# A spectral-filter and token-mixing kernel on Trainium2: a leaner first stage, and six filter scans moved into the filter stage

## The chip, the cores and the metric

The kernel runs on one core of one Trainium2 chip. The core has five engines that run their own instruction streams side by side: TensorE (PE, matrix products into PSUM, with its weight loads as PEld), VectorE (DVE), ScalarE (ACT), GpSimd (POOL) and SyncE (SP, which here only issues transfers). They wait for one another through semaphores, and each takes its instructions strictly in its own order: an instruction that waits holds back all that stands behind it on that engine. The metric is the device time of one execution in microseconds (us). Three runs of the kernel before gave a median of 1017.25 us (1016.85 to 1018.95).

## The reference

The input x has S = 2048 tokens by D = 640 channels. Two kinds of layer alternate, each twice, and each adds its result to x:

```python
def _A_ref(x, w_r, w_i):
    X = rfft2(x);  X = X * (w_r + 1j * w_i)          # filter: 2048 x 321 complex numbers
    return irfft2(X, s=(S, D))

def _B_ref(x, w1, b1, w2, b2):                        # MLP over the token axis, F = 1728
    u = gelu(einsum("bsd,sf->bdf", layernorm(x), w1) + b1)
    return transpose(einsum("bdf,fs->bds", u, w2) + b2)

x = x + _A_ref(_layernorm(x), w_r, w_i)
x = x + _B_ref(_layernorm(x), w1, b1, w2, b2)
x = x + _A_ref(_layernorm(x), w_r, w_i)
x = x + _B_ref(_layernorm(x), w1, b1, w2, b2)
```

## The kernel before, in words

The two-dimensional transform is done as matrix products with tables of cosines and sines, in pairs of float16 parts (a high part and a low part, which carries what the high one lost by rounding). The program is written in stages: the first stage (in `run`), and then twice: the filter stage `a1`, the inverse transform `a2`, and the MLP (`b1st`, `b2nd`).

**The first stage** works on 16 rows of tiles (128 tokens by 640 channels). It is pipelined by hand: step i of the loop `for i in range(NJ + 6)` loads x of row i+3, computes the mean and variance `mv` of row i on DVE, v (variance plus epsilon, ACT), r (its inverse root, POOL), nm (the negative mean, ACT) and nb (nm times r, POOL) of row i-1, the normalised z of row i-2 (ACT), the first fold of row i-3 (`a0_fold1`: `eo`, sums and differences of the two halves of z, POOL), the second fold of row i-4 (`a0_fold2`: `f`, DVE), the float32 products with the table tM of row i-5 (PE), and the split of the result into the float16 parts s1h (ACT) and s1l (DVE) of row i-6. Both folds end with a small copy of two columns that have no partner. `eo` and `f` have two buffers each. Every z is a fresh tile, whose two pad columns POOL clears.

Between those, the first stage reads the filter: for each of its 16 groups a **scan** loads the group's filter (`w`, 321 KB, on SP's queue) and lets ACT sum its squares into one column of `xq` (the tile `jw` takes the squares, which nobody reads). From all of `xq`, `scale_x` in group 0 of the filter stage makes the scales `sx` and a correction `cxe`: a product of `xq` with the identity `eye` on PE turns the columns into rows, DVE takes the maxima (`xm`), spreads them (`xb`), a second product with `eye` turns them back, and a chain of small DVE steps (`xqq`, `qi`, `sx`, `xof`, `cxe`) makes powers of two of them.

**The filter stage** works in groups g = 0 to 15. In group g stand, in this order: the products d of group g+1 (PE), the inverse products i of g-3, the products s of g (PE, from ph and pl), then xh, xl of g-2, the filter products ta and tb of g-1 (DVE, which read s's result in PSUM, the scale sx and the filter w), their sums sa, sb (POOL), the split ph (ACT) and pl (DVE) of the d result of g+1, and Yh (ACT), Yl (DVE) of the i result of g-3. In groups 4 to 7 small steps for the scale of the MLP's bias (`scale_b`) are put between; one of them is a product of `sqb` with a column of ones on PE, which goes to a spare column of the newest s result's PSUM tile.

**What sets the order.** Around the change nothing is reordered: the work is pinned in the order in which the program issues it, each engine's part of it in that order. All transfers named here go through SP's one queue. All instructions of the engines record the same line (L59, in the kernel after it L60), that of a helper, so that one goes by tiles.

Of the kernel before, what the change touches and what calls it, by code (L numbers as in the profile page):

```python
# [22 lines left out]
NX = 5  # L23
LAST = '''
# [42 lines left out]
class Layers:  # L67
# [156 lines left out]
    def scan_x(self, pool, g):  # L224

        w = self.t(pool, [128, 2, NL], F32, "w", 3)
        self.nc.sync.dma_start(w, self.A["w"][g])
        junk = self.t(pool, [128, 2, NL], BF16, "jw", 1)
        return lambda: self.T.activation(junk, w, AF.Square, accum_out=self.xq[:, g:g + 1])

    def scale_x(self, pool):

        V, mm = self.V, self.PE.matmul
        ps = self.big()
        mm(ps[:NG, 0, :128], self.xq, self.eye, start=True, stop=True)
        m = pool.tile([NG, 1], F32, name="xm")
        V.tensor_reduce(m, ps[:NG, 0, :128], op=ALU.max, axis=mybir.AxisListType.X)
        yield
        b = pool.tile([NG, 128], F32, name="xb")
        V.tensor_copy(b, m.to_broadcast([NG, 128]))  # L240
        mm(ps[:, 1, :NG], b, self.eye[:NG, :NG], start=True, stop=True)
        yield
        q = pool.tile([128, NG], F32, name="xqq")
        V.tensor_scalar(q, ps[:, 1, :NG], SMALL, XS ** -2, op0=ALU.max, op1=ALU.mult)
        i = self.pow2(q, self.sx)
        V.tensor_scalar(q, i, EC * 0.5 / TS, None, op0=ALU.mult)
        yield
        of = pool.tile([128, NG], F32, name="xof")
        V.tensor_reduce(of, self.eye.rearrange("p (g a) -> p g a", g=NG), op=ALU.add, axis=mybir.AxisListType.X)
        V.tensor_tensor(of, of, q, op=ALU.mult)  # L250
        V.tensor_reduce(self.cxe, of, op=ALU.add, axis=mybir.AxisListType.X)
# [64 lines left out]

    def a0_fold1(self, z, sv=False):
# [10 lines left out]
    def a0_fold2(self, eo, between=lambda: None, gp=False):  # L328

        V, W = self.V, self.G if gp else self.V  # L330
# [10 lines left out]
        W.tensor_copy(f[:, 607:640:32], eo[:, 160:482:321])  # L341
# [92 lines left out]
    def a1(self, first):  # L434
# [232 lines left out]
        spare = lambda c: lambda: ps2[max(ps2)][:, 1, c:c + 1]  # L667
        for g in range(NG - 3):
            for op in group(g):
                do(op)  # L670
                if op == "pl%d" % (g + 1) and 9 <= g < 13:
                    self.wsplit(0, quarter(g - 9)[0], hi=False, part=quarter(g - 9)[1])
                if op == "d1" and first:
                    sx = self.scale_x(p)
# [9 lines left out]
            if g > 0 and g + 2 < NG:  # L684
                w[g + 2] = wload(g + 2)
            if g == 3:
# [984 lines left out]
    def run(self):  # L1671
# [9 lines left out]
        scans = []  # L1681
        x, st, z, eo, f, pv, vs, nms = ({} for _ in range(8))

        def load(i):
            if i < NJ:
                x[i] = self.t(self.pT, [128, D], F32, "xt", 6)
                self.lastld = nc.sync.dma_start(x[i], self.xs[0][i])
                if i % 4 == 0:
# [273 lines left out]
```

## Time and profile before

| | |
|---|---|
| median of 3 runs | 1017.25 us (1016.85 to 1018.95) |
| the profiled execution | 1017.07 us, of which the span of the profile is 1015.3 us |
| PE busy | 969.4 us (95% of the span), 8235 products |
| DVE, ACT, POOL busy | 781.8 us (77%), 576.5 us (57%), 300.0 us (30%) |
| chain that ended last | PE 36%, DVE 13%, ACT 6%, POOL 3%, DMA 2% of the span |
| mean granted clock of PE | 0.979 |
| transfers | 176.45 MB, mean 174 GB/s |

How to read what follows: a row of a timeline has the start (us from the span's start), the duration, the engine, the line, the operation, its output and input tiles with their sizes, how many instructions the row joins, and in brackets how long the engine had been idle before it and what ended that. A row of a table of windows has each engine's busy time in that stretch, the number of its instructions in brackets, then the clock that PE was granted (1.00 is full speed), the share of the DMA engines' time and what they moved.

### The profile page before, as it was taken

The numbers are of one execution on the slowest core, as the hardware profiler recorded it, in microseconds if no ns is written. First come the engines' busy times: TensorE is split into PE (matmuls) and PEld (weight loads), VectorE is DVE, ScalarE is ACT, GpSimd is POOL, SyncE is SP. The second block draws the span as 40 slices with busy tenths as digits, with TensorE's granted clock in tenths as the row PEclk, the third lists the DMA queues.
The fourth block names the chain that finished last, engine by engine and source line by source line (L and its number), as shares of the span: only waits on it lengthen the run. The fifth ranks groups of instructions, "written<-read, shape, count | busy, mean of one in ns | idle before, by whom it ended". The sixth has DMA issues, their size and how long they took to land.

```text
span 1015.3 us, 20992 instructions
## 1 busy us (share of the span) xinstructions
PE 969.4 (95%) x8235; PEld 721.2 (71%) x8235; DVE 781.8 (77%) x1493; ACT 576.5 (57%) x890; POOL 300.0 (30%) x502
## 2 busy tenths in 40 slices
PE   4889999999999999999999799999999999999998
PEld 3778777677777667777777688776777777677776
DVE  7978978988777784666666689789965557998885
ACT  5857668687666455555553377685643454544531
POOL 6937857412212201222222277574000000000000
PEclk9599999999999999999999999999999999999999
DMA  7865356557657546464423455365444446755411
GB/s 232 279 185 164 115 178 219 206 187 255 236 195 250 186 124 246 139 193 146 126 89 117 126 181 181 105 229 204 159 156 164 145 142 228 245 177 190 153 45 53
DMA packets 67259, 176.45 MB, mean 174 GB/s; under 512 B 7996, under 2 KB 15320, under 8 KB 67160
## 3 DMA queue, kind: packets, MB, share of 16 engines
q1 hardware_dynamic: 59384, 146.92, 45.1%
q0 software_dynamic: 7776, 28.20, 7.5%
q8 instruction: 64, 1.05, 0.4%
q14 instruction: 35, 0.29, 0.1%
HBM read 127.24 MB, written 47.84 MB: 172 GB/s over the span
## 4 chain that ended last, share of the span: by engine, by line
PE 36%; DVE 13%; ACT 6%; POOL 3%; issue 3%; DMA 2%; SPq 0%; ACTq 0%; DVEq 0%; POOLq 0%
PE ps L59 36%; DVE wl L59 3%; DMA xt<-x 2%; DVE st L59 2%; DVE xt L59 1%; POOL eo L59 1%; DVE f L59 1%; ACT wh L59 1%; ACT xt L59 1%; ACT z L59 1%; DVE s1l L59 1%; ACT junk L59 1%; POOL xt L59 1%; DVE Yl L59 1%; DVE S L59 1%
## 5 line engine op out<-in xcount | busy, mean ns | idle before, releaser
L59 PEld LDWEIGHTS <-wh 128*128 128x128 f16 x2602 | 251.9, 98 | 103.6 <-issue 5.0
L59 PEld LDWEIGHTS <-wl 128*128 128x128 f16 x1610 | 157.5, 98 | 66.0 <-DVE wl L59 2.8
L59 PE MATMUL ps<-ul,wh 128*128 128x320 f16 x448 | 133.9, 301 | 0.6 <-DVE ul L59 0.6
L59 PE MATMUL ps<-uh,wl 128*128 128x320 f16 x448 | 133.9, 301 | 0.1
L59 PE MATMUL ps<-uh,wh 128*128 128x320 f16 x416 | 124.8, 300 | 1.6 <-DVE s L59 1.6
L59 PE MATMUL ps<-hl,wh 128*128 128x320 f16 x496 | 102.2, 299 | 0.9 <-DVE hl L59 0.9
L59 PEld LDWEIGHTS <-wo 128*128 128x128 f16 x756 | 73.9, 98 | 29.4 <-DVE wo L59 0.8
L59 DVE SCALAR_TENSOR_TENSOR wl<-raw,s,wh 128x896 f16<-128x896 f32 (+2 forms) x64 | 75.0, 1176 | 12.9 <-ACT wh L59 12.7
L59 ACT ACTIVATE junk<-raw 128x896 bf16<-128x896 f32 (+1 forms) x60 | 59.5, 991 | 44.2 <-DMA raw<-w 44.0
L59 POOL TENSOR_TENSOR r<-v,mh 128x1 f32<-128x1 f32 x64 | 36.4, 569 | 158.4 <-DVE nm L59 149.0
L59 PE MATMUL ps<-tDi,Yh 128*128 128x322 f16 x320 | 71.3, 300 | 0.2
L59 DVE TENSOR_TENSOR f<-eo 128x256 f32<-128x256 f32 (+1 forms) x124 | 39.1, 368 | 40.7 <-POOL eo L59 40.1
L59 ACT ACTIVATE wh<-raw,s 128x896 f16<-128x896 f32 (+2 forms) x68 | 67.2, 1010 | 2.3 <-DVE s L59 1.6
L59 POOL TENSOR_TENSOR xt<-xt,ec 128x320 f32<-128x320 f32 x64 | 52.5, 842 | 34.2 <-DVE xt L59 34.0
L59 ACT ACTIVATE z<-xt,nb,r 128x640 f32<-128x640 f32 x31 | 28.5, 919 | 57.6 <-POOL z L59 45.3
L59 PE MATMUL ps<-ph,tS 128*128 128x321 f16 (+2 forms) x288 | 58.5, 286 | 1.3 <-DVE tb L59 1.3
L59 PE MATMUL ps<-u,wo 128*128 128x320 f16 x420 | 59.0, 299 | 0.5 <-DVE wo L59 0.5
L59 DVE BATCH_NORM_STATS2 st<-xt 128x6 f32<-128x320 f32 x126 | 55.3, 480 | 5.2 <-DMA xt<-x 4.5
L59 PE MATMUL ps<-hha,wh 128*128 128x320 f16 x288 | 58.1, 299 | 0.9 <-DVE wh L59 0.9
L59 POOL TENSOR_TENSOR eo<-z 128x320 f32<-128x320 f32 x62 | 53.3, 881 | 17.0 <-ACT z L59 15.1
L59 PE MATMUL ps<-tM,f 128*128 128x128 f32 x160 | 39.5, 426 | 19.6 <-DVE f L59 19.6
L59 PE MATMUL ps<-tDi,Yl 128*128 128x322 f16 x192 | 55.7, 299 | 1.7 <-DVE Yl L59 1.7
(251 smaller groups left out, 2376.6 us busy)
## 6 DMA issues: line engine op xcount, KB each, us to landing
xt<-x SPq DMA_DIRECT2D x79, 320.0 KB
raw<-w SPq DMA_DIRECT2D x32, 512.0 KB
w<-w SPq DMA_DIRECT2D x48, 321.0 KB
x<-xt SPq DMA_DIRECT2D x47, 320.0 KB
raw<-w SPq DMA_DIRECT2D x32, 448.0 KB
raw<-w2z SPq DMA_DIRECT2D x32, 448.0 KB
w1S<-sp POOLq DMA_DIRECT2D x20, 512.0 KB, 3.7
out<-xt SPq DMA_DIRECT2D x15, 320.0 KB
```

Source lines behind the costliest of these rows:

```text
L59: i = f(*a, **k)
```

## The change

1. In the first stage, the two small copies go to ACT: a new function `a0_eo` takes the place of `a0_fold1`, and `a0_fold2` is called with `act=True`. nm falls away; nb is made by one POOL step from the mean and r. The z tiles are two fixed ones, whose pads are cleared once.
2. The order on ACT within a step is now s1h, z, copy of eo, v, copy of f, scan; row 0 is folded, and its products are issued, one step sooner (`soon`); the first part of the table tM is loaded behind x of row 2 instead of row 0.
3. The first stage holds ten scans, one in every second step and two behind the loop. The other six are done in the groups 0 to 5 of the filter stage: their loads on SP behind the group's loads, their ACT work at the group's end.
4. `scale_x` is done in two parts: columns 0 to 9 in group 0, where all of it stood, and columns 10 to 15 in group 6. There the first product with `eye` and the maximum stand behind s6, the spread and the second product behind ta5, the powers behind Yl3, all in spare columns of s6's PSUM tile; `xof` and `cxe` end that group.

ACT in the first stage, one step of the loop before (s1h to the scan's `jw`):

```order
L59 ACTIVATE s1h_195<-ps_430 128x80x8
L59 ACTIVATE nm_474<-mv_449 128x1
L59 ACTIVATE v_473<-mv_449,eps 128x1
L59 ACTIVATE z_487<-xt_282,nb_457,r_455 128x640
L59 ACTIVATE jw_422,xq<-w_420 128x642
```

and two steps of it now, one without and one with a scan:

```order
L60 ACTIVATE s1h_195<-ps_406 128x80x8
L60 ACTIVATE z_220<-xt_282,nb_432,r_430 128x640
L60 ACTIVATE eo_452<-z_219 128x2
L60 ACTIVATE v_456<-mv_424,eps 128x1
L60 ACTIVATE f_461<-eo_412 128x2
L60 ACTIVATE s1h_195<-ps_446 128x80x8
L60 ACTIVATE z_219<-xt_306,nb_472,r_470 128x640
L60 ACTIVATE eo_487<-z_220 128x2
L60 ACTIVATE v_491<-mv_464,eps 128x1
L60 ACTIVATE f_496<-eo_452 128x2
L60 ACTIVATE jw_476,xq<-ws_474 128x642
```

nm is gone, v stands behind z, and the copies of eo and f are in ACT's row.

ACT at the beginning of the filter stage, before (the last scan of the first stage, ph of groups 0, 1 and 2, xh of group 0):

```order
L59 ACTIVATE jw_858,xq<-w_856 128x642
L59 ACTIVATE ph_929<-ps_904 128x321 x2
L59 ACTIVATE ph_964<-ps_935 128x2x321
L59 ACTIVATE ph_1032<-ps_1009 128x2x321
L59 ACTIVATE xh_219_878<-ta_1026 128x2x321
```

and now:

```order
L60 ACTIVATE jw_764,xq<-ws_762 128x642
L60 ACTIVATE ph_845<-ps_820 128x321 x2
L60 ACTIVATE ph_887<-ps_857 128x2x321
L60 ACTIVATE jw_853,xq<-ws_851 128x642
L60 ACTIVATE ph_954<-ps_931 128x2x321
L60 ACTIVATE jw_856,xq<-ws_854 128x642
L60 ACTIVATE xh_175_794<-ta_948 128x2x321
```

A scan stands ahead of ph of group 2, and another ahead of the first xh.

DVE in group 6, before (ta and tb of group 5, pl of group 7, Yl of group 3, ta of group 6):

```order
L59 SCALAR_TENSOR_TENSOR ta_1445<-ps_1333,sx,w_1180 128x642
L59 SCALAR_TENSOR_TENSOR tb_1447<-ps_1333,sx,w_1180 128x642
L59 SCALAR_TENSOR_TENSOR pl_1452<-ps_1375,ph_1451 128x2x321
L59 SCALAR_TENSOR_TENSOR Yl_872<-ps_1392,Yh_871 128x96x4 x2
L59 SCALAR_TENSOR_TENSOR ta_1533<-ps_1429,sx,w_1274 128x642
```

and now, up to the first of the small steps on xqq:

```order
L60 TENSOR_REDUCE xm_1379<-ps_1365 6x1
L60 SCALAR_TENSOR_TENSOR ta_1384<-ps_1268,sx,w_1110 128x642
L60 COPY xb_1386<-xm_1379 6x128
L60 SCALAR_TENSOR_TENSOR tb_1389<-ps_1268,sx,w_1110 128x642
L60 SCALAR_TENSOR_TENSOR pl_1394<-ps_1311,ph_1393 128x2x321
L60 SCALAR_TENSOR_TENSOR Yl_788<-ps_1328,Yh_787 128x96x4 x2
L60 TENSOR_SCALAR xqq<-ps_1365 128x6
```

The maximum xm stands ahead of ta of group 5, the copy between ta and tb, and xqq behind Yl.

PE in group 6, before (the last product of s6, the product with ones, the first product of d8):

```order
L59 MATMUL ps_1429<-ph_1355,tS_198 128x321
L59 LDWEIGHTS ones
L59 MATMUL ps_1429<-sqb_278_1371,ones 128x1
L59 LDWEIGHTS s1h_195
L59 MATMUL ps_1463<-tD_197,s1h_195 128x160
```

and now, behind the last product of s6, with the semaphore on which each waits:

```order
L60 MATMUL ps_1365<-eye,xq 6x128 [waits Activation_49]
L60 MATMUL ps_1365<-eye,xb_1386 128x6 [waits DVE_49]
L60 LDWEIGHTS ones
L60 MATMUL ps_1365<-sqb_246_1307,ones 128x1 [waits DVE_49]
L60 LDWEIGHTS s1h_195
L60 MATMUL ps_1416<-tD_197,s1h_195 128x160 [waits PE_49]
```

Two products that depend on ACT and DVE stand between s6 and the product with ones, all three in s6's PSUM tile.

The diff, cut to its core:

```diff
-        w = self.t(pool, [128, 2, NL], F32, "w", 3)
+        w = self.t(pool, [128, 2, NL], F32, "ws", 2)
...
-    def scale_x(self, pool):
...
+    def scale_x(self, pool, cs, at=None):
+
+        V, mm, n = self.V, self.PE.matmul, cs.stop - cs.start
+        if not cs.start:
+            self.xqq = pool.tile([128, NG], F32, name="xqq")
+            ps = self.big()
+            at = (lambda: ps[:, 0, :128]), (lambda: ps[:, 1, :n])
+        a = at[0]()[:n]
+        mm(a, self.xq[:, cs], self.eye, start=True, stop=True)
+        m = pool.tile([n, 1], F32, name=f"xm{n}")
+        V.tensor_reduce(m, a, op=ALU.max, axis=mybir.AxisListType.X)
         yield
+        b = pool.tile([n, 128], F32, name=f"xb{n}")
+        V.tensor_copy(b, m.to_broadcast([n, 128]))
+        a = at[1]()[:, :n]
+        mm(a, b, self.eye[:n, :n], start=True, stop=True)
         yield
+        q = self.xqq[:, cs]
+        V.tensor_scalar(q, a, SMALL, XS ** -2, op0=ALU.max, op1=ALU.mult)
+        i = self.pow2(q, self.sx[:, cs])
         V.tensor_scalar(q, i, EC * 0.5 / TS, None, op0=ALU.mult)
         yield
+        if cs.stop == NG:
...
+    def a0_eo(self, z):
+
+        G = self.G
+        eo = self.t(self.pT, [128, 646], F32, "eo", 2)
+        v2 = lambda a, o, w: a[:, o:o + 2 * w].rearrange("p (a b) -> p a b", a=2)[:, :, 0:160]
+        za, zb = v2(z, 1, 161), v2(z, 321, 160)
+        G.tensor_tensor(v2(eo, 1, 161), za, zb, op=ALU.add)
+        self.lastpool = G.tensor_tensor(v2(eo, 322, 161), za, zb, op=ALU.subtract)
+        self.T.activation(eo[:, 0:162:161], z[:, 0:162:161], AF.Copy)
+        return eo
...
-        W.tensor_copy(f[:, 607:640:32], eo[:, 160:482:321])
+        if act:
+            self.T.activation(f[:, 607:640:32], eo[:, 160:482:321], AF.Copy)
+        else:
+            V.tensor_copy(f[:, 607:640:32], eo[:, 160:482:321])
...
-        spare = lambda c: lambda: ps2[max(ps2)][:, 1, c:c + 1]
+        spare2 = lambda c, e: lambda: ps2[max(ps2)][:, 1, c:e]
+        spare = lambda c: spare2(c, c + 1)
+        more = [self.scan_x(p, k) for k in (NX1, NX1 + 1)] if first else []
         for g in range(NG - 3):
             for op in group(g):
                 do(op)
+                if first and g == 6 and op in ("s6", "ta5", "Yl3"):
+                    if op == "s6":
+                        sx = self.scale_x(p, slice(NX1, NG), (spare2(328, 456), spare2(460, 460 + NG - NX1)))
+                    next(sx)
...
                 if op == "d1" and first:
-                    sx = self.scale_x(p)
+                    sx = self.scale_x(p, slice(0, NX1))
...
+            if more:
+                more.pop(0)()
+                if NX1 + 2 + g < NG:
+                    more.append(self.scan_x(p, NX1 + 2 + g))
+            if first and g == 6:
+                next(sx)
...
-                if i % 4 == 0:
-                    nc.sync.dma_start(self.tM[i // 4], A["tM32"][:, i:i + 4])
+                if i % 4 == 0 and i or i == 2:
+                    nc.sync.dma_start(self.tM[i // 4], A["tM32"][:, i // 4 * 4:i // 4 * 4 + 4])
...
+        zs = [self.pT.tile([128, 642], F32, name=f"z{i}") for i in range(2)]
+        for q in zs:
+            self.G.memset(q[:, D:], 0.0)
...
+            self.G.tensor_scalar(b, st[k][:, 0:1], r, -1.0, op0=ALU.mult, op1=ALU.mult)
...
+            if len(scans) and i % 2 == 0:
                 scans.pop(0)()
+            if i > 4 and len(got) < NX1 and (i % 2 or i > 14):
+                got.append(i)
+                scans.append(self.scan_x(pw, len(got) - 1))
```

79 lines of the change are left out of this document (35 added, 44 removed).

## The prediction

> **What bounds the kernel now.** I read the page's first two parts, then a table of windows, then a timeline of each place that the change touches.
>
> ```profile
> PE 969.4 (95%) x8235; PEld 721.2 (71%) x8235; DVE 781.8 (77%) x1493; ACT 576.5 (57%) x890; POOL 300.0 (30%) x502
> ```
>
> ```profile
> core 0: us, PE busy (x) PEld busy (x) DVE busy (x) ACT busy (x) POOL busy (x), PEclk, DMA share, GB/s
> 0.00:60.00 60.00, 39.59 (x162) 34.32 (x162) 52.18 (x147) 40.24 (x92) 44.39 (x100) 0.72 0.75 240
> 60.00:70.00 10.00, 9.45 (x102) 7.74 (x102) 6.05 (x17) 4.31 (x10) 0.00 (x0) 1.00 0.67 221
> 70.00:80.00 10.00, 9.61 (x144) 7.79 (x142) 7.77 (x12) 5.63 (x12) 7.25 (x9) 1.00 0.54 146
> 80.00:90.00 10.00, 10.00 (x154) 8.20 (x151) 8.61 (x15) 8.64 (x19) 9.12 (x11) 1.00 0.76 248
> 90.00:100.00 10.00, 9.80 (x170) 7.99 (x170) 9.27 (x21) 7.17 (x16) 6.38 (x8) 1.00 0.45 125
> ```
>
> TensorE (PE) is busy for 95% of the span. Only the first 60 us, the first stage, have another limit: PE works 39.59 of 60, at a clock of 0.72. From 80 on PE has next to no idle time (0.20 in 20 us, and 5% over the whole span with the first stage in it), so what it loses there stays lost; what the first stage gains is kept if the groups behind it follow.
>
> The limit of the first stage is a loop over three engines. One row, by the timeline:
>
> ```profile
> 41.15 1.69 POOL L59 TENSOR_TENSOR eo<-z 128x320 f32<-128x320 f32 x2 [0.17 <-DVE f L59]
> 42.44 0.81 DVE L59 TENSOR_TENSOR f<-eo 128x256 f32<-128x256 f32 x2
> 42.78 0.38 POOL L59 COPY eo<-z 128x2 f32<-128x2 f32 x1
> 43.16 0.54 POOL L59 TENSOR_TENSOR r<-v,mh 128x1 f32<-128x1 f32 x1
> 43.29 0.50 DVE L59 TENSOR_TENSOR f<-eo 128x256 f32<-128x256 f32 x2
> 43.52 0.28 ACT L59 ACTIVATE v<-mv,eps 128x1 f32<-128x1 f32 x1
> 43.78 0.19 POOL L59 TENSOR_TENSOR nb<-nm,r 128x1 f32<-128x1 f32 x1
> 43.83 0.17 DVE L59 COPY f<-eo 128x2 f32<-128x2 f32 x1
> 44.01 0.92 ACT L59 ACTIVATE z<-xt,nb,r 128x640 f32<-128x640 f32 x1 [0.20 <-POOL nb L59]
> 44.14 0.87 POOL L59 TENSOR_TENSOR eo<-z 128x320 f32<-128x320 f32 x1 [0.17 <-DVE f L59]
> ```
>
> The row lasts 44.14 - 41.15 = 2.99 us. POOL's two big eo operations take 1.69; DVE's first f pair, issued at 42.44, comes out only at 43.25, when they have long ended; the second pair ends at 43.79, its small copy at 44.00, and 0.14 later POOL, which waits for that eo buffer, begins the next row.
>
> **The change, part by part.** The sum is made against the profiled execution's 1017.07 us (span 1015.3), 0.18 below the median of 1017.25.
>
> *Start.* The table tM[0] is loaded behind x2 instead of behind x0; the two z pads are cleared once.
>
> ```profile
> 3.96 0.89 DVE L59 BATCH_NORM_STATS2 st<-xt 128x6 f32<-128x320 f32 x2 [2.90 <-DMA xt<-x]
> 6.67 0.89 DVE L59 BATCH_NORM_STATS2 st<-xt 128x6 f32<-128x320 f32 x2 [1.58 <-DMA xt<-x]
> 10.96 0.56 DVE L59 TENSOR_TENSOR f<-eo 128x256 f32<-128x256 f32 x2 [0.28 <-POOL z L59]
> ```
>
> Rows 0 and 1 arrive 2.71 us apart, with the 256 KB of tM between them and the 320 KB of x1; 256/576 of that is 1.2. Row 0's z stands on ACT behind row 1's v and POOL's nb, so it moves by the whole 1.2; POOL's clearing of a pad (0.28 at 10.96) goes too. That is -1.4, the first f at 9.5. That row 0 is folded, and its products are issued, a step sooner needs no further term: its chain of z, eo, f is what the 1.4 shifts. Row 0's products need tM[0] themselves: behind x2, with 1.5 for x2's and 1.2 for its own bytes, it lands near 6.7 - 1.2 + 2.7 = 8.2, ahead of f. Bounds: 0 if x1 takes as long without tM, -1.8 if f also gains the time of POOL's small eo copy (0.38, above).
>
> *Rows.* POOL loses the 0.38 copy, and nb, now the mean times r times -1 in one step, takes 0.27 by the row below, where it took 0.19. ACT loses nm and gains two copies of two columns. The one for f now frees the eo buffer.
>
> ```profile
> L59 POOL TENSOR_SCALAR nb<-mv,r x32: 267/267/1610, 143.6 to 699.4; 128x1 f32<-128x1 f32 x32
> 57.17 0.70 ACT L59 ACTIVATE s1h<-ps 128x640 f16<-128x640 f32 x1 [2.16 <-PE ps L59]
> 61.58 0.74 ACT L59 ACTIVATE jw<-w 128x642 bf16<-128x642 f32 x1 [0.16 <-DMA w<-w]
> ```
>
> The part of the loop through DVE keeps its length: 43.79 + 0.04 to start + 0.19 + 0.08 to POOL (a small ACT operation and ACT-to-POOL hand-over, estimates from this trace's other ones) is 44.10 where it was 44.14. So a row without a scan stays near 2.96: the copy that leaves POOL lay beside DVE's pair, so its 0.38 is worth nothing to the loop. A row with a scan has on ACT 0.70 (s1h) + 0.92 (z) + 0.19 + 0.28 (v) + 0.19 + 0.74 (scan) = 3.02, with the read-out of the scan's sum (0.19) 3.21, and now f's copy is in that queue, with the eo buffer and POOL behind it: 3.2. Scans come every second step, so the mean row is 3.08, +0.09 over 10 rows: +0.9. Bounds: POOL's own chain of 1.69 + 0.54 + 0.27 + 0.17 = 2.67 gives -0.32 a row, -3.5 over 11 rows; +0.2 a row, every row at ACT's sum, gives +2. I take +0.9, nearest to the loop that the trace shows closed. Ten scans instead of 16 relieve ACT only where it waits anyhow. The last rows, without loads or stats, stay: 0.
>
> *Fill of the filter stage.* Scans 10 and 11 are loaded by SP behind the third w load; before, that queue had no scan there.
>
> ```profile
> 58.62 0.33 SPq L227 DMA_DIRECT2D w<-w  x1
> 67.67 0.36 SPq L492 DMA_DIRECT2D w<-w  x1
> 69.50 0.71 ACT L59 ACTIVATE ph<-ps 128x642 f16<-128x642 f32 x1 [4.58 <-PE ps L59]
> 67.73 0.28 DVE L59 TENSOR_REDUCE xof<-eye 128x16 f32<-128x128 f32 x1
> 68.34 0.88 DVE L59 SCALAR_TENSOR_TENSOR ta<-ps,sx,w 128x642 f32<-128x642 f32 x1
> ```
>
> The last scan's load took 61.58 - 58.62 = 2.96 from issue to use. Issued at 68.1, less the 0.6 of the new lead, the new one lets its scan start at 70.4, and ACT's ph of group 2 stands behind that scan (the order of ACT is shown with the change): 71.2 instead of 69.50 - 0.6 = 68.9, 2.3 late. PE waits for pl behind ph. In 60 to 80 PE has 0.94 idle, which takes that much of it; three small DVE operations (xof, cxe) leave the way to the first ta, 68.34 - 67.73 = 0.61 sooner. So 2.3 - 0.9 - 0.6 = +0.8; bounds 0 (the scan's data is there in time) and +1.6.
>
> *Group 6, second half of the scale.* Here the main term lies. Prices, from the first half's place and from group 6 of before:
>
> ```profile
> 64.11 0.39 PE L59 MATMUL ps<-eye,xq 128*16 128x128 f32 x2
> 64.53 0.28 DVE L59 TENSOR_REDUCE xm<-ps 16x1 f32<-16x128 f32 x1
> 65.69 0.20 DVE L59 COPY xb<-xm 16x128 f32<-16x128 f32 x1
> 66.60 0.17 DVE L59 TENSOR_SCALAR xqq<-ps 128x16 f32<-128x16 f32 x1 [0.70 <-PE ps L59]
> 86.17 0.88 DVE L59 SCALAR_TENSOR_TENSOR ta<-ps,sx,w 128x642 f32<-128x642 f32 x1
> 88.55 0.83 DVE L59 SCALAR_TENSOR_TENSOR pl<-ps,ph 128x642 f16<-128x642 f32 x1 [0.71 <-ACT ph L59]
> 89.29 1.01 DVE L59 SCALAR_TENSOR_TENSOR Yl<-ps,Yh 128x384 f16<-128x384 f32 x2
> 90.22 0.88 DVE L59 SCALAR_TENSOR_TENSOR ta<-ps,sx,w 128x642 f32<-128x642 f32 x1
> 88.73 0.17 PE L59 MATMUL ps<-sqb,ones 128*128 128x1 bf16 x1
> 88.76 0.30 PE L59 MATMUL ps<-tD,s1h 128*128 128x160 f16 x2
> ```
>
> DVE's xm waits for PE's s6, which ends at 88.73, and stands ahead of ta5, which ran at 86.17: everything of DVE moves behind it. xm ends at 88.73 + 0.42 (64.11 to 64.53) + 0.28 = 89.43; ta5 to 90.22 (DVE starts the next 0.80 later); then xb's copy, at 90.22; PE's second product, which reads it, is to be had 66.60 - 65.69 = 0.91 later, at 91.1. DVE meanwhile goes on in its order: tb5 to 91.1, pl7 to 91.8 (0.74, 88.55 to 89.29), the two Yl to 92.8 (0.93, 89.29 to 90.22); only then comes xqq, which reads that product. PE's one-column product with ones writes into the same PSUM tile and waits for xqq; behind it on PE is d8. So d8 starts at 92.76 + 0.17 + 0.08 = 93.01, where it started at 88.76: +4.2. DVE's next ta follows xqq by the seven small steps, 68.34 - 66.60 = 1.74: 94.5 instead of 90.22, also +4.2. Bounds: +2.5, if PE's one-column product doesn't wait and DVE alone (xm's delay of 88.73 + 0.7 - 86.17 = 3.3, less what it waited, 0.71) is late; +5.
>
> *The six scans on ACT* in groups 1 to 5: ACT has 1.4 of 10 us free in 80:90, 2.8 in 90:100, and a scan takes 0.74 and its read-out in a group: 0, at most +0.8. Their loads go over SP's queue behind each group's stk and w loads, one of 0.36 us more in a group; the w loads that follow are wanted two groups later, which covers it.
>
> *The clock.*
>
> ```profile
> 52.00:55.00 3.00, 1.70 (x11) 1.00 0.62 140
> 56.00:58.00 2.00, 2.00 (x12) 0.50 0.92 267
> ```
>
> (Windows of PE alone: PE busy, granted clock.) After 3 us with 1.3 idle the clock is halved soon after, for some 3.3 us. In the stall of group 6 PE is idle for 1.35 (to xm and xb) and 2.1 of 4.25. I take +0.8, half of a full 1.65 lost; bounds 0 and +1.7. The Trainium skill, "TensorE: Matmul & The Clock Gate", section "Part 1: The HAM clock gate (the "warmup" mystery)", says that the clock is halved after an idle window of about 3.4 us; by it both pauses are too short and the sum would be 1021.2, but the fall after 1.3 us of idle time above does not agree with it.
>
> *Later waits* take back some: PE's 0.20 idle in 90:100 and the like: -0.3.
>
> Sum: -1.4 + 0.9 + 0.0 + 0.8 + 4.2 + 0 + 0.8 - 0.3 = +5.0; 1017.07 + 5.0 = 1022.1. The fill's term is the softest, so I say 1022.0.
>
> **The rivals.**
> 1. Clock holds and the stall is the whole loss: no 0.8, 1021.2; with the rows at 2.96 throughout, 1020.3. For it: in 52:55 the idle time ended a stage of which PE had worked 39.59 of 60, while here it comes out of 10.00 of 10; against it, the clock stood at 1.00 there too until the fall. 0.20.
> 2. Other side: the rows do run at POOL's pace. If DVE's first pair gets in earlier because POOL's 0.38 copy no longer follows the eo pair, 2.67 a row gives -1.4 - 3.5 + 0.8 + 4.2 = +0.1, 1017.2, not slower; at 2.5 a row it would be faster. It decides where rows fall under 2.82 (below +2). Against it: f's second pair starts at 43.29, before r, so the copy delayed nothing of DVE's. 0.10, and 0.07 for rows still faster or a start that gains more.
> 3. The stall is smaller, since DVE's wait is taken up by PE's slack: +2.5 - 1.3, 1018.4 to 1019.5. Against it: PE has 10.00 of 10 in 80:90. 0.08.
> 4. ACT with six scans is late for ph and Yh in every group: 6 x 0.9 more, 1026. ACT's 8.64 in 80:90 speaks for it, the 7.17 after against. 0.05.
>
> **How the numbers follow.** The forecast, with a stall of 4 and one or the other clock term, has 0.50. The range of 8 in 10 reaches from the small stall with a good first stage, 1018.6, to the upper bounds of fill and clock, 1025.0. About 2.0 us (0.2%) is what tells from no change. Slower: forecast 0.50, rival 1 0.20, most of 3 (0.08), rival 4 0.05: 0.83. Same: 0.10. Faster: 0.07.
>
> **What would show it.** Rows in the new profile: first f near 9.5; eo to eo alternating between 2.96 and 3.2; ACT's scan waiting for its DMA ahead of ph near 70; DVE idle ahead of xm, near 88, for over 2 us, and PE idle twice ahead of d8, 1.3 and 2.1; PEclk at half after it. The forecast is wrong if rows come at 2.7, if the one-column product doesn't wait for xqq, or if d8 follows s6 at once.

## The result, and the profile after

The changed kernel takes 1027.06 us (median of 6 runs, 1025.76 to 1029.45) where the kernel before takes 1017.72 (6 runs): a ratio of 1.0093, 95% interval 1.0077 to 1.0108, 9.3 us slower. Slower was forecast, at 1022.0 with a range up to 1025.0: the sign held, the forecast size was about half of the measured one.

Windows of the kernel after, columns as in the windows of before:

```profile
0.00:60.00 60.00, 40.24 (x155) 34.19 (x156) 52.85 (x130) 37.00 (x95) 42.82 (x70) 0.75 0.61 198
60.00:70.00 10.00, 8.66 (x83) 6.80 (x82) 5.14 (x14) 4.44 (x10) 0.00 (x0) 0.97 0.72 240
70.00:80.00 10.00, 7.45 (x103) 6.08 (x102) 6.13 (x8) 5.79 (x14) 4.47 (x6) 1.00 0.82 245
80.00:90.00 10.00, 10.00 (x152) 8.28 (x150) 8.51 (x14) 9.06 (x23) 9.12 (x11) 1.00 0.87 243
90.00:100.00 10.00, 6.56 (x95) 5.11 (x95) 6.26 (x17) 6.35 (x13) 4.71 (x5) 0.91 0.52 174
```

ACT has less to do in the first 60 us (37.00 against 40.24), POOL too (42.82 against 44.39), yet the stage isn't shorter. PE loses time in 60:80 (16.11 busy against 19.06) and in 90:100 (6.56 against 9.80).

To say where, the same work is looked up in both traces and the difference of the starts taken. This table has it for the kernel after and for the runs told of below (us, behind the kernel before in its profiled execution; ahead of it where negative): the first f of row 4, and PE's first product d of a group, by its place in the kernel before.

```
                        row 4's f   d at 59.9   d at 80.7   d8 at 88.8   d at 113.3   ratio of medians
after                     +1.35       +1.92       +4.26        +8.55        +9.56      1.0093
tM[0] back                +0.84       +0.70       +3.43        +7.73        +9.73      1.0088
row 0 late                -1.11       +0.46       +3.29        +7.59        +8.59      1.0088
v first                   -0.12       -1.37       +1.11        +5.41        +7.59      1.0071
late scale                +1.25       +1.11       +4.17        +4.17        +8.70      1.0075
stage 1 alone             +1.29       +2.66       +3.95        +3.95        +3.91      1.0031
scans alone               +0.02       +0.91       +4.28        +8.58        +9.57      1.0070
PE filled                 +0.98       +1.87       +3.39        +7.94        +8.60      1.0064
v first, all scans        -1.30       -1.85       -0.42        -0.42        -0.42      0.9997
all scans, early          -0.90       +0.81       +2.19        +2.19        +2.20      1.0015
late scale, free fill     +1.27       +1.10       +1.82        +1.82        +7.29      1.0043
all scans, in the tail    -1.29       +0.86       +2.41        +2.41        +2.39      1.0045
ones sooner               +1.18       +1.04       +3.24        +6.55        +8.00      1.0089
```

So the kernel after stands 1.9 behind at the end of the first stage, loses 2.3 more in the fill, 4.3 in group 6 and 1.0 behind it: 9.5, near the 9.3 by which the medians differ. The profiled execution itself took 1029.39, 2.3 above the median; its difference grows to 12.3 at the end. Of that, 1.9 come between 560 and 590 us, where PE waits in every kernel here and its clock falls in one execution more than in another (the same +2 is in the runs "row 0 late" and "v first", it is missing in "tM[0] back" and "scans alone"), so it isn't the change's. Runs of one kernel lie as much as 7 us apart, too ("all scans, in the tail", 1018.61 to 1025.86), and the medians of most of the kernels below can't be told from that of the change; the places in the traces therefore carry more of what follows than the medians.

The places scatter as well. "PE filled", "late scale", "late scale, free fill" and "ones sooner" have the changed first stage unaltered. Their row 4 stands at +0.98 to +1.27 and their d at 59.9 at +1.04 to +1.87, beside +1.35 and +1.92 of the change. In the two executions at +1.9 PE's granted clock was 0.50 in 58:60, in the three at +1.0 to +1.1 it was 1.00, so that some 0.8 of the 1.9 go with the clock of one execution. The fill (d at 59.9 to d at 80.7) cost 2.34 in the change and 1.52, 3.06 and 2.20 in the three kernels that share it unaltered up to there but for a few small steps, on average 2.3.

**The start.** Row 3's statistics and row 4's first f on DVE, before:

```profile
8.79 0.83 DVE L59 BATCH_NORM_STATS2 st<-xt 128x6 f32<-128x320 f32 x2
23.91 1.22 DVE L59 TENSOR_TENSOR f<-eo 128x256 f32<-128x256 f32 x2
```

DVE and POOL in the timeline of the kernel after, and three windows of it:

```profile
6.55 0.89 DVE L60 BATCH_NORM_STATS2 st<-xt 128x6 f32<-128x320 f32 x2 [0.46 <-DMA xt<-x]
9.89 0.89 DVE L60 BATCH_NORM_STATS2 st<-xt 128x6 f32<-128x320 f32 x2 [2.11 <-DMA xt<-x]
10.52 1.89 POOL L60 TENSOR_TENSOR eo<-z 128x320 f32<-128x320 f32 x2
10.70 1.79 DVE L60 TENSOR_TENSOR f<-eo 128x256 f32<-128x256 f32 x2
25.26 1.22 DVE L60 TENSOR_TENSOR f<-eo 128x256 f32<-128x256 f32 x2
```

```profile
5.00:6.00 1.00, 0.00 (x0) 0.00 (x0) 0.97 (x4) 0.29 (x1) 0.48 (x1) 1.00 0.73 74
6.00:7.00 1.00, 0.00 (x0) 0.00 (x0) 0.54 (x3) 0.83 (x2) 0.83 (x3) 1.00 0.69 146
...
9.00:10.00 1.00, 0.00 (x0) 0.00 (x0) 0.10 (x1) 0.57 (x2) 0.52 (x2) 1.00 1.04 411
```

x1 does arrive sooner (its statistics start at 5.02, not 6.67), but x3, behind tM[0], comes only at 9.89, where its statistics started at 8.79 before. Row 0's f, a step sooner now, stands on DVE behind the statistics of that row 3. It starts at 10.70, not 9.5, and just behind POOL's next eo (10.52), so that it lasts 1.79 us where it lasted 0.56. The DMA engines are busy for 70% in 5:7 and move 74 and 146 GB/s. By 5 us they had moved 0.98 MB, the bytes of x0 to x2, so the 0.22 MB of 5:7 are most of tM[0]: behind x2 it is a slow transfer, and x3 waits behind it.

**The rows.** From the timeline, POOL's eo, v on ACT and r on POOL in two rows, with the scan's `jw` in the first:

```profile
39.56 0.72 ACT L60 ACTIVATE jw<-ws 128x642 bf16<-128x642 f32 x1
39.74 1.71 POOL L60 TENSOR_TENSOR eo<-z 128x320 f32<-128x320 f32 x2
41.77 0.28 ACT L60 ACTIVATE v<-mv,eps 128x1 f32<-128x1 f32 x1
42.13 0.55 POOL L60 TENSOR_TENSOR r<-v,mh 128x1 f32<-128x1 f32 x1 [0.69 <-ACT v L60]
43.00 1.99 POOL L60 TENSOR_TENSOR eo<-z 128x320 f32<-128x320 f32 x2
44.05 0.28 ACT L60 ACTIVATE v<-mv,eps 128x1 f32<-128x1 f32 x1
44.96 0.54 POOL L60 TENSOR_TENSOR r<-v,mh 128x1 f32<-128x1 f32 x1
45.94 1.71 POOL L60 TENSOR_TENSOR eo<-z 128x320 f32<-128x320 f32 x2
```

Rows take 3.26 and 2.94 by turns, from one eo to the next. After the scan POOL stands idle for 0.69 until v comes, 42.13; in the other row r follows eo at once. The eo buffer is free by then; it is v that is late.

**The fill.** SP, ACT and PE around group 2:

```profile
69.62 0.91 SPq L228 DMA_DIRECT2D ws<-w  x2
73.04 0.74 ACT L60 ACTIVATE jw<-ws 128x642 bf16<-128x642 f32 x1 [6.20 <-DMA ws<-w]
73.78 0.69 ACT L60 ACTIVATE ph<-ps 128x642 f16<-128x642 f32 x1
75.38 0.30 PE L60 MATMUL ps<-pl,tS 128*128 128x321 f16 x1 [0.56 <-DVE pl L60]
```

**Group 6.** DVE, PE and POOL, from the timeline:

```profile
93.50 0.28 DVE L60 TENSOR_REDUCE xm<-ps 6x1 f32<-6x128 f32 x1 [3.62 <-PE ps L60]
94.76 0.38 PE L60 MATMUL ps<-eye,xb 6*128 6x6 f32 x2 [1.30 <-DVE xb L60]
97.09 0.14 DVE L60 TENSOR_SCALAR xqq<-ps 128x6 f32<-128x6 f32 x1
97.28 0.16 PE L60 MATMUL ps<-sqb,ones 128*128 128x1 bf16 x1 [2.14 <-DVE xqq L60]
97.89 1.43 POOL L60 TENSOR_TENSOR xl<-ta,xh 128x642 f16<-128x642 f32 x1 [0.85 <-ACT xh L60]
98.09 1.26 DVE L60 TENSOR_SCALAR xqq<-qi 128x6 f32<-128x6 f32 x1
99.90 0.89 DVE L60 SCALAR_TENSOR_TENSOR ta<-ps,sx,w 128x642 f32<-128x642 f32 x1
```

The two pauses of PE are 1.30 and 2.14 us, in the places and with the releasers that were forecast. The clock around them (windows of PE alone, granted clock behind PE's time; the windows are cut where the clock of this trace changes, and 3.41 us ahead of that):

```profile
91.30:94.71 3.41, 2.16 (x18) 1.00 0.83 267
94.71:98.12 3.41, 1.22 (x15) 1.00 0.30 98
98.12:101.53 3.41, 3.41 (x46) 0.50 0.02 5
```

### The profile page after: what moved, and what is told of

It is laid out like the page before. It is cut to its first block, busy times and chain, and to the rows that moved or that the text cites. A ratio compares the mean times of both kernels' runs of the same rounds, so it can differ in the third digit from the quotient of the medians.

```text
span 1027.6 us, 20954 instructions
## 1 busy us (share of the span) xinstructions
PE 975.5 (95%) x8239; PEld 724.0 (70%) x8239; DVE 785.6 (76%) x1485; ACT 578.5 (56%) x906; POOL 297.5 (29%) x472
## 4 chain that ended last, share of the span: by engine, by line
PE 37%; DVE 10%; ACT 5%; DMA 4%; POOL 3%; issue 2%; SPq 0%; ACTq 0%; POOLq 0%; DVEq 0%
PE ps L60 37%; DMA xt<-x 4%; DVE wl L60 3%; DVE st L60 1%; DVE xt L60 1%; ACT wh L60 1%; ACT z L60 1%; POOL xt L60 1%; DVE s1l L60 1%; POOL eo L60 1%; ACT junk L60 1%; ACT xt L60 1%; DMA raw<-w2z 1%; DVE f L60 1%; DVE S L60 1%
## 5 line engine op out<-in xcount | busy, mean ns | idle before, releaser
L60 DVE TENSOR_TENSOR f<-eo 128x256 f32<-128x256 f32 (+1 forms) x124 | 44.7, 413 | 40.1 <-POOL eo L60 40.1
```

Source lines behind the costliest of these rows:

```text
L60: i = f(*a, **k)
```

## The experiments

**tM[0] back behind x0**, all else as in the change:

```diff
-                if i % 4 == 0 and i or i == 2:
+                if i % 4 == 0:
```

> Only tM[0]'s load goes back to behind x0. Theory A (the slow transfer of tM[0] now stands ahead of x3, and DVE's statistics of row 3 with it ahead of row 0's fold): row 3's statistics start near 8.8 us instead of 9.89, row 0's first f near 10.3 instead of 10.70, the first f of row 3 near 20.5 instead of 22.00, the first filter-stage product 1 to 1.5 us sooner than its 61.82, the time near 1025.8. Theory B (the early fold of row 0 itself brings POOL and DVE out of step): row 3's first f stays at 21.5 or later and the time near 1027.

1025.2 us; ratio 1.0088 (1.0060 to 1.0116), by which it can't be told from the change. DVE of this kernel:

```profile
9.08 0.83 DVE L60 BATCH_NORM_STATS2 st<-xt 128x6 f32<-128x320 f32 x2
11.08 0.56 DVE L60 TENSOR_TENSOR f<-eo 128x256 f32<-128x256 f32 x2 [1.17 <-POOL eo L60]
```

Row 3's statistics no longer wait for data, and f is at its short 0.56 again. But row 0's f starts later, at 11.08 (10.3 was expected), and row 3's at 21.48, so row 4 is late by 0.84 where the five kernels with the changed first stage have 0.98 to 1.35, and the first filter-stage product by 0.70 where they have 1.04 to 1.92. Theory A holds for the data; in time it is worth some 0.1 to 0.5 at row 4, hardly more than those five scatter.

**Row 0 at its ordinary step**, tM[0] behind x2:

```diff
-        soon = lambda i, k: [j for j in ((0,) if i == k - 1 else (i - k,)) if 0 < j < NJ or j == 0 and i == k - 1]
+        soon = lambda i, k: [i - k] if 0 <= i - k < NJ else []
```

> Only row 0 is folded at its ordinary step again; tM[0] stays behind x2. Theory A: row 0's f now waits for x4 too, it starts at 12 or later, nothing is gained, 1027 to 1028.5. Theory B: rows come in the undisturbed rhythm, 2.8 us for the first three, the first f of row 3 near 20, the first filter-stage product near 60.5, 1025.5.

1025.71 us; ratio 1.0088 (1.0070 to 1.0107). DVE, first f of rows 3 and 4:

```profile
19.82 0.99 DVE L60 TENSOR_TENSOR f<-eo 128x256 f32<-128x256 f32 x2
22.80 1.21 DVE L60 TENSOR_TENSOR f<-eo 128x256 f32<-128x256 f32 x2
```

Theory B: with row 0 late, row 4 comes at 22.80 where the changed kernel has 25.26, and where the kernel before had 23.91. With the changed order on ACT, the early fold of row 0 costs 2.5 us by row 4. So the first rows of the change do gain on the kernel before as long as row 0 isn't folded early. What tM[0]'s move has of that gain, and what the copies have, wasn't separated. (At row 8 ACT waited 1.88 for a scan's load and the row took 5.35, so neither the places from there on nor the median show the gain.)

**v ahead of z on ACT** again (v first):

```diff
+            if has[1] and i != 2:
+                var(i - 1)
             if has[2]:
                 z[i - 2] = zs[i % 2]
...
-            if has[1] and i != 2:
-                var(i - 1)
             if has[0]:
```

> On ACT v stands ahead of z and of eo's copy again, all else as in the changed kernel. Theory A (in a step after a scan, v comes late, so r, nb and POOL's next eo come late): rows no longer alternate between 2.99 and 3.21, all take about 2.99; 0.11 less on some 9 rows, the first filter-stage product 1.0 sooner, 60.8, the time near 1026. Theory B (as predicted: f's copy on ACT stands behind the scan and holds the eo buffer): rows go on alternating, 1027.

1024.56 us; ratio 1.0071 (1.0053 to 1.0089). POOL of this kernel:

```profile
37.62 1.71 POOL L60 TENSOR_TENSOR eo<-z 128x320 f32<-128x320 f32 x2 [0.19 <-ACT f L60]
40.62 1.72 POOL L60 TENSOR_TENSOR eo<-z 128x320 f32<-128x320 f32 x2 [0.19 <-ACT f L60]
```

Theory A: all rows take 3.00, and the first filter-stage product comes at 58.53, 3.3 sooner than in the changed kernel and 1.4 sooner than before. That is more than the 1.0 expected, since the first rows gained too: row 4's f comes at 23.79 where the change has 25.26. Row 0 is folded early here as well, so its early fold costs less with v first; the two losses of the first rows aren't independent. At 80.7 us, though, the kernel is 1.1 behind again. Of the 2.5 us, 1.5 are lost before d at 68.2, where the granted clock is 0.50 (60:62), and 1.0 behind it, where scan 10 waits on ACT for its load until 69.75, ahead of ph of group 2.

**The second half of the scale in groups 9 and 10** (late scale):

```diff
-                if first and g == 6 and op in ("s6", "ta5", "Yl3"):
-                    if op == "s6":
+                if first and op in ("s9", "Yl6", "s10", "Yl7"):
+                    if op == "s9":
...
-            if first and g == 6:
+            if first and g == 10:
                 next(sx)
```

(with the maximum and the copy moved behind Yl6, by two more pauses in `scale_x`).

> The second half of the scale is done in groups 9 and 10, behind the steps of the bias scale: first product with the identity behind s9, maximum and copy behind Yl6, second product behind s10, powers behind Yl7, xof and cxe at the end of group 10. Theory A (in group 6 PE waits for DVE in a ring, and the clock falls behind it): the two pauses of PE, 1.30 and 2.14 us, are gone, the granted clock stays at 1.00 between 88 and 106 us, ta of group 6 follows at 3.6 to 3.9 us behind the one of before instead of 9.7, the time falls by 5.5 to 6, to about 1021.3. Theory B (the six scans and their loads in the groups are what costs): no more than 1 to 2 us come back, 1025 to 1026.

1024.82 us; ratio 1.0075 (1.0049 to 1.0101). Group 6 costs nothing now: +4.17 ahead of it and behind it, and the clock stays at 1.00 there. But only a third of what was expected comes back, because the loss moves to group 10. DVE and PE of this kernel, and windows of PE alone:

```profile
112.69 1.26 DVE L60 TENSOR_SCALAR qi<-sx 128x6 int32<-128x6 int32 x1
116.41 0.32 PE L60 MATMUL ps<-tD,s1h 128*128 128x160 f16 x2 [2.01 <-DVE tb L60]
```

```profile
114.60:118.01 3.41, 1.60 (x28) 1.00 0.20 50
118.01:121.42 3.41, 3.41 (x38) 0.50 0.25 68
```

There PE waits 2.01 for DVE's tb (d goes from 4.24 behind at 97.1 to 8.70 at 113.3, of which 1.4 come back by 140 us; the last 1.5 of it fall where the clock is halved behind that wait): from 100 to 120 us DVE was 9.63 and 10.00 of 10 busy already before the change, and the split scale brings it 2.8 us of small steps, one of them again 1.26 long. Neither theory saw that: the ring in group 6 is real, and DVE has no room for the steps in groups 9 and 10 either.

**The first stage alone:** the changed first stage, but all 16 scans in it, one a step and with three buffers for their loads as before, and the scale whole in group 0.

```diff
-NX1 = 10
+NX1 = 16
...
-                if first and g == 6 and op in ("s6", "ta5", "Yl3"):
...
-            if len(scans) and i % 2 == 0:
-                scans.pop(0)()
-            if i > 4 and len(got) < NX1 and (i % 2 or i > 14):
-                got.append(i)
-                scans.append(self.scan_x(pw, len(got) - 1))
+            if 6 <= i < NG + 6:
+                scans.append(self.scan_x(pw, i - 6))
+            if i >= 8 and scans:
+                scans.pop(0)()
```

> The first stage as changed (copies on ACT, nb in one step, fixed z tiles, row 0 sooner, tM[0] behind x2, v behind z), but all 16 scans in it, one a step as before, and the scale whole in group 0. Theory A (two causes, each in its own place): rows of 3.2 us throughout, because every step now has a scan ahead of v; the first filter-stage product at 62 to 63, 2.5 later than before; no pause of PE in group 6, no scan ahead of ph in the fill; time near 1019.5. Theory B (the stages' losses are one, scans moved late): the first stage alone is no slower than before, 1017.5.

1021.06 us (10 runs); ratio 1.0031 (1.0014 to 1.0048), +3.2. Rows with a scan in each take 3.21, the first filter-stage product is 2.66 later, and nothing is lost in group 6. Theory A. The loss is 0.9 larger than expected: between d at 59.9 and d at 68.2 another 1.3 are lost, where the last scan waits 1.50 for its load, until 66.21, ahead of the first ph.

**The scans alone:** the first stage of before (its copies, nm, order on ACT), with ten scans in it, six in the groups and the scale in two parts, by the same lines as in the change's diff.

> The first stage as before (its copies, nm, order on ACT, tM[0] behind x0), with ten scans in it and six in groups 0 to 5, and the scale in two parts as changed. Theory A: the first stage takes as long as before (first filter-stage product at 59.5 to 60), the fill loses 0.8 to 1.7, group 6 loses 5.9 with its two pauses of PE and the half clock; time near 1024.5. Together with the run of the first stage alone the two losses, 2.3 and 7, make up the change's 9.3. Theory B (ten scans free ACT in the first stage): it becomes faster by 1 or more, time 1023.

1024.54 us; ratio 1.0070 (1.0044 to 1.0095), +7.0. Until 32 us this kernel follows the one before to 0.02; freeing ACT of six scans gains nothing there, against theory B. Then a scan waits for its load until 33.34, and that row takes 3.76. The fill loses 3.4: ph of group 2 is 2.2 late beside the stage's end, and 1.2 more are lost while the granted clock is 0.50 (74:76). Group 6 loses 4.3. By the medians the two halves of the change cost 3.2 and 7.0 alone, 10.2 in sum, where both together cost 9.3; but the 7.0 may be anything from 4.5 to 9.7, and by the places this kernel is as far behind at 113.3 (9.57) as the whole change. That the two halves add up isn't shown.

**PE filled in its pauses,** with products that nobody reads:

```diff
+        def idle(n):
+            for _ in range(n):
+                mm(ps2[6][:, 0, 328:489], self.tS2[:, 0, 0, 0], self.tD[:, 0], start=True, stop=True)
...
                     next(sx)
+                    if op != "Yl3":
+                        idle(13 if op == "s6" else 28)
```

> The changed kernel with products on PE that nobody reads, 13 behind the first product with the identity in group 6 and 28 behind the second, written to unused columns: PE works through its two pauses, the waits of DVE stay. Theory A (the half clock behind the pauses costs PE 1.7 us that it doesn't get back): the granted clock stays at 1.00 from 98 to 102 us, the drift behind the kernel before falls from 9.5 to about 7.8 at 110 us, time near 1025.3. Theory B (after the stall DVE is the limit, and the slow PE lies beside it): the clock stays up but the drift stays within 0.5 of 9.5, time near 1027.

1024.53 us; ratio 1.0064 (1.0040 to 1.0088). Windows of PE alone:

```profile
98.00:100.00 2.00, 2.00 (x44) 1.00 0.00 0
100.00:102.00 2.00, 0.97 (x9) 1.00 0.01 4
```

The clock stays at 1.00, so the pauses are what halved it. But it hardly helps: from d at 84.7 to d at 113.3 this kernel loses 5.21 us (3.39 to 8.60), the changed one 5.31. PE at full speed waits later, 1.03 us in 100:102, for DVE's pl. That is nearer to theory B. The products themselves delay DVE, though: from xm to the next ta it takes 6.78 (92.64 to 99.42) instead of 6.40 (93.50 to 99.90). And in the changed kernel the next d, which has to wait for that pl too, starts at 102.84, 0.5 behind pl's end at 102.32. So the half clock costs between 0.1 and 0.5 us there. (The lower median comes from the fill, 0.9, and from between 200 and 400 us, where the edit changes nothing.)

**The ones product sooner:** the bias scale one group earlier, so that its product isn't behind the second product with `eye`.

```diff
-            if first and g == 4:
+            if first and g == 3:
                 sb = self.scale_b(at=spare(400))
-            if first and 4 <= g < 8:
+            if first and 3 <= g < 7:
                 next(sb)
```

> The changed kernel with the steps of the bias scale one group sooner, so that the one-column product with ones stands in group 5 and not behind the second product with the identity in group 6. Theory A (DVE's order is the binding one: ta of group 6 stands behind xqq and the small steps whatever PE does): PE's pause of 2.14 us goes from ahead of d8 to a later place, DVE's ta of group 6 stays at 9 to 9.7 behind the kernel before, the time falls by less than 1, to 1026 to 1027. Theory B (PE's wait is the binding one): PE is 2.1 less behind from d8 on, time near 1025.

1025.11 us; ratio 1.0089 (1.0068 to 1.0111). PE and DVE of this kernel:

```profile
95.31 0.32 PE L60 MATMUL ps<-tD,s1h 128*128 128x160 f16 x2 [1.15 <-DVE pl L60]
98.94 0.88 DVE L60 SCALAR_TENSOR_TENSOR ta<-ps,sx,w 128x642 f32<-128x642 f32 x1
99.08 0.30 PE L60 MATMUL ps<-ph,tS 128*128 128x321 f16 x1 [1.35 <-DVE qb L60]
```

```profile
93.57:96.98 3.41, 2.06 (x34) 1.00 0.35 100
```

Theory A: PE's wait for xqq is gone, and 1.15 and 1.35 of waiting for DVE stand in its place. Groups 6 and behind cost 4.8 (3.24 to 8.00) instead of 5.3. DVE takes 6.43 from xm to the next ta, as in the change (6.40). So PE's ring and DVE's order were two chains of nearly one length; cutting one gains half a microsecond. The clock stays at 1.00 in this kernel (the window shown has its two pauses of 1.30 and 1.15), so the half clock may have a part in that gain.

**The late scale and a free fill:** as the late scale, and each of the six scans one group later.

```diff
-            if more:
+            if more and g > 0:
                 more.pop(0)()
-                if NX1 + 2 + g < NG:
-                    more.append(self.scan_x(p, NX1 + 2 + g))
+                if NX1 + 1 + g < NG:
+                    more.append(self.scan_x(p, NX1 + 1 + g))
```

> The changed kernel with the second half of the scale in groups 9 and 10, as in the run with the late scale, and each of the six scans in the groups one group later, so that none stands ahead of ph of group 2. Theory A (the scan that waits for its load ahead of ph makes the fill's whole loss): in the fill ph of group 2 follows at the first stage's 1.9 behind the kernel before instead of 4.2, that lead over the late-scale run of 2.3 us stays, and the time is near 1022.5. Theory B (PE's idle time in the groups behind the fill had hidden part of it, or the loads of the scans delay the w loads): less than 1 comes back, 1024.

1022.2 us; ratio 1.0043 (1.0022 to 1.0064). ACT of this kernel:

```profile
71.23 0.71 ACT L60 ACTIVATE ph<-ps 128x642 f16<-128x642 f32 x1 [4.68 <-PE ps L60]
72.78 0.74 ACT L60 ACTIVATE jw<-ws 128x642 bf16<-128x642 f32 x1 [0.83 <-DMA ws<-w]
```

Theory A: ph waits for PE again and not for a scan, and the kernel is 1.82 behind at 80.7 us, not 4.17. From d at 59.9 the fill loses 0.7 here and 3.1 in the late-scale run: the scan ahead of ph was 2.3 of it.

**The first stage repaired** (v first, all scans): the changed first stage with v first, row 0 at its ordinary step, all 16 scans in it and the scale whole (the edits of "row 0 late", "v first" and "stage 1 alone").

> The first stage as changed, but v ahead of z on ACT again and row 0 folded at its ordinary step, all 16 scans in it and the scale whole in group 0. Theory A (each loss has been named: v behind the scan, row 0's early fold, the fill, group 6): first f's of rows 3 and 4 near 19.8 and 22.8, rows of 2.99 behind, the first filter-stage product near 58.3, and from there the kernel before's course, 1.5 sooner: time 1016.0, faster than before by 0.15%. Theory B (the first stage gains nothing that the filter stage doesn't give back): 1017.5.

1017.74 us (12 runs) beside 1017.9 of the kernel before; ratio 0.9997 (0.9981 to 1.0013): the same. The stage ends 1.85 ahead, and 1.4 of that go again at its last scan:

```profile
61.82 0.74 ACT L60 ACTIVATE jw<-ws 128x642 bf16<-128x642 f32 x1 [1.59 <-DMA ws<-w]
```

**The same, scans two steps sooner** (all scans, early):

```diff
-            if 6 <= i < NG + 6:
-                scans.append(self.scan_x(pw, i - 6))
-            if i >= 8 and scans:
+            if 4 <= i < NG + 4:
+                scans.append(self.scan_x(pw, i - 4))
+            if i >= 6 and scans:
```

> The kernel with v first, row 0 at its ordinary step and all 16 scans in the first stage, with each scan loaded and summed two steps sooner, so that the last load doesn't stand behind the end of the stage. Theory A (the first stage's lead of 1.9 us is given back only because the last scan's load lands at 61.8, near the same time as before): the first ph at about 61.0 instead of 62.6, PE stays 1.5 to 1.9 ahead of the kernel before through the filter stage, time 1016.0 to 1016.5. Theory B (scans beside the first rows slow x's loads): rows 3 to 8 fall behind by 1 or more and nothing is gained, 1017.5.

1019.29 us (12 runs); ratio 1.0015 (1.0003 to 1.0027). Theory B, though by another way than x's loads: a scan waits for its own data on ACT, and z, queued behind it, makes POOL's next eo 2.4 us late (39.25; 3.00 behind the eo before it would be 36.84):

```profile
36.56 0.74 ACT L60 ACTIVATE jw<-ws 128x642 bf16<-128x642 f32 x1 [2.80 <-DMA ws<-w]
```

Another 1.4 are lost between d at 59.9 and d at 68.2, where the granted clock is 0.50 (62:64).

**The same, two scans a step at the end** (all scans, in the tail):

```diff
+            for k in range(1 if i < 15 else 2):
+                if i >= 6 and len(got) < NG:
+                    got.append(i)
+                    scans.append(self.scan_x(pw, len(got) - 1))
+            for k in range(1 if i < 17 else 2):
+                if i >= 8 and scans:
+                    scans.pop(0)()
```

> The kernel with v first, row 0 at its ordinary step and all 16 scans in the first stage; the scans begin as before, but from step 15 on two are loaded in a step and from step 17 on two are summed, where no x is loaded any more. Theory A (the lead of 1.9 us was given back at the last scan's load alone): no scan waits ahead of the first ph, which comes at 61.0 to 61.3, PE stays 1.4 to 1.9 ahead of the kernel before from 68 us on, time near 1016.3. Theory B (something else holds the filter stage's start at its place, the tables or rest): the first ph at 62.5 again, 1017.5.

1021.19 us (12 runs); ratio 1.0045 (1.0028 to 1.0061). Rows run as forecast until 54 us, 1.9 ahead; then scans wait for their loads ahead of s1h, and PE behind s1h. ACT and PE:

```profile
57.61 0.74 ACT L60 ACTIVATE jw<-ws 128x642 bf16<-128x642 f32 x1 [0.73 <-DMA ws<-w]
60.76 0.45 PE L60 MATMUL ps<-tD,s1h 128*128 128x160 f16 x2 [4.12 <-ACT s1h L60]
```

No scan waits ahead of the first ph, but ph itself comes only at 64.78, and PE's clock has a part in that: behind the wait of 4.12 it is 0.50 in 60:64, and another 1.5 us are lost between d at 59.9 and d at 68.2. "tM[0] back", "v first" and "all scans, early" lose 1.4 to 1.5 at the same place and clock; the kernels with ten scans and a clock of 1.00 there lose 0.0 to 0.4. Neither theory fits. That the loads of 16 filters set the end of this stage as much as its rows do is read from the waits of three kernels and wasn't tested by itself; nor was another place for the last two scans.

## Why the prediction was wrong in size

Its terms, and what the traces put in their place:

- **Start, -1.4: failed.** Measured +1.35 at row 4. The step "That row 0 is folded ... a step sooner needs no further term" was wrong by the most: it costs 2.5 ("row 0 late"), because f of row 0 moved behind the statistics of row 3 on DVE and into POOL's next eo. The step "256/576 of that is 1.2" moved x1 and forgot that x3 now stood behind the slow table. The place of v, which the prediction didn't price, has a part here too: with v first, row 4's f comes at 23.79 with row 0 early and at 22.61 with it late, so that the early fold costs 1.2 there.
- **Rows, +0.9:** measured +0.57 from row 4 to the stage's end. The rhythm of 2.96 and 3.2 was right (2.94 and 3.26 from eo to eo), its cause was not: v, which had been moved behind z and so further behind the scan, and not f's copy that holds the buffer ("v first"). The prediction listed v's move in the order but gave it no price.
- **Fill, +0.8:** mis-sized; 2.3 measured. ph was 2.3 late, as worked out; the two subtractions, 0.9 for PE's idle time and 0.6 for the small DVE steps, were not there. The whole 2.3 arrived at PE (d goes from 1.92 to 4.26) and stayed; "late scale, free fill" brings 2.3 back. Idle time that a table of windows shows for 20 us isn't there at the place where a delay enters.
- **Group 6, +4.2: right.** 4.3, with both pauses to within 0.05 us, and the same 4.3 in "tM[0] back", "row 0 late", "v first" and "scans alone", whatever came before.
- **Clock, +0.8, and later waits, -0.3:** 0.5 together, where 1.0 was measured behind d8. The clock does fall to 0.50, for 3.41 us, but costs only 0.1 to 0.5 ("PE filled"). The rest is DVE, which the prediction let go on at +4.2: its next ta stands 9.68 behind the kernel before (99.90), 5.4 more than ahead of group 6. From xqq to that ta the small steps took 2.81 where the prediction had 1.74, because the last step on xqq took 1.26 instead of 0.17 beside POOL's xl. The Trainium skill, "TensorE: Matmul & The Clock Gate", section "Part 1: The HAM clock gate (the "warmup" mystery)", has the clock halved after an idle window of some 3.4 us. By that rule it would have stayed at full speed behind pauses of 1.30 and 2.14; the trace disagrees if such a window has to be free of all work, since PE worked 1.22 us in the 3.41 ahead of the fall.
- **Scans on ACT, 0:** right where they stand behind the group's work; the one that stood ahead of ph is the fill's term.

The sum of the measured terms, 1.92 + 2.34 + 4.29 + 1.01 = 9.56, agrees with the 9.3 of the medians. Of the 4.6 that the prediction fell short (9.56 against its 5.0), 2.4 are the first stage (1.92 where it had -0.5; about 0.8 of the 1.92 go with the clock of that execution), 1.5 the fill and 0.5 what follows group 6. That the execution shown comes so near to the medians is in part luck, as its places scatter by 1 us from one execution to the next.

Of the rivals, the first (clock holds) and the third (slack takes up the stall) are refuted, and so is the fourth (ACT late in every group): from d at 80.7 to d at 84.7, with the scans in the groups, the shift stays at 4.26 and 4.25. The second, rows at POOL's pace of 2.67, doesn't come either: with v first rows run at 3.00 (the last ones at 2.77, as at 2.79 before), POOL waiting for the release of eo's buffer by ACT's copy of f.

## What to carry to other kernels

When an instruction moves a step sooner in a pipeline, it must be followed on every queue that it enters: ask which load the instruction ahead of it waits for. On an engine that runs in order, work with slack that waits for a load (here the scan) is harmless only behind the work that others wait for; ahead of it, it passes its whole wait on. And a small chain taken out of a stage with idle engines and put into one where DVE is at 9 of 10 cost 3.1 to 5.3 us in each of the three arrangements tried (group 6, group 6 with the ones product sooner, groups 9 and 10).

## What the runs showed of the hardware

- The 256 KB of tM[0] pass slowly behind x2, right at the start: 74 and 146 GB/s in 5:7, with the DMA engines busy for 70%, where 411 GB/s are moved a little later (9:10). The statistics of x3, behind it, started 3.34 us after those of x2 (6.55 to 9.89). The cause of the slow stretch stays open.
- A DVE step on 6 columns took 1.26 us, not 0.17, beside POOL's xl, and ended with it (99.35 and 99.32). One step of the chain, not always the same, does so in all nine kernels with the scale in two parts, for 1.26 to 1.40 us. The Trainium skill, "GPSIMD Engine Reference", section "8. Key points", says that POOL shares its SBUF interfaces with VectorE and contends with those of its instructions that use a 2-port mode or two SBUF inputs. The trace agrees that there is such contention, and doesn't show the mode of the step.
- The granted clock changes on a grid of 3.41 us, which lies elsewhere in every execution. In the kernel after, it changes at 26.44, 29.85, 60.57, 98.12 and 101.53 us, that is 1, 9, 11 and 1 times 3.41 apart. It fell behind stretches of this grid in which PE worked 1.22 us (94.71:98.12) and, in the late scale, 1.60 with a single pause of 2.01 (114.60:118.01); it held behind 2.06 in "ones sooner" (93.57:96.98). Over the whole traces, stretches with 1.5 to 2.0 us of work are found with a fall behind them and without, so this isn't a sharp limit.
- What the half clock went with: 0.1 to 0.5 us behind group 6 of the kernel after, where DVE is nearly as late as PE, and 1.4 to 1.5 us at the first products of the filter stage in "tM[0] back" and "v first".
